# Loading the first batch's q and k by whole tokens and turning them on the matrix engine, with a new order of instructions, in a clustered-attention and SoLU feed-forward kernel

## The chip, the cores and the metric

One core of a Trainium2 chip runs the kernel. The metric is the time of one execution on the device in microseconds (us), the median of several runs; lower is better. The profile of one execution gives in addition the span, from its first to its last instruction, and for each engine what ran when. The engines are PE (matrix multiplication; PEld is its loading of the stationary operand), DVE (vector), ACT (activation), POOL and SP, which issues most transfers.

## The reference

```python
B, H, S, D = q.shape                      # 4, 8, 768, 64; 16 clusters a head
q_n = q / (norm(q) + 1e-6); k_n = k / (norm(k) + 1e-6); c_n = centroids / (norm(centroids) + 1e-6)
q_assign = argmax(einsum('bhsd,hcd->bhsc', q_n, c_n)); k_assign = argmax(einsum('bhsd,hcd->bhsc', k_n, c_n))
scores = where(q_assign[..., :, None] == k_assign[..., None, :], q @ k.T / 8, -1e9)
attn_out = softmax(scores) @ v
x = attn_out.transpose(0, 2, 1, 3).reshape(3072, 512)
h = x @ w_in                              # 512 to 1024
solu = h * softmax(h)
ln = (solu - mean(solu)) / sqrt(var(solu) + 1e-6) * g_ln
out = ln @ w_out                          # 1024 to 512
```

A key counts for a query only if both fall to the same centroid of their head. The sum over keys does not depend on the order of the keys, as long as k and v have the same order.

## The kernel before, in words

**Attention.** The work is cut into 4 batches and, in each, 4 pairs of heads. For each pair, q and k (`i` is 0 for q, 1 for k) are brought in as `raw`, laid out so that a transposition of 32x32 blocks on DVE (`turn`, L297) gives `xt`: 128 partitions, the 64 numbers of the one head above the 64 of the other, by 768 tokens in fp32. Four transfers fill a `raw` (`load`, L289), each of 96 KB in pieces of 32 numbers, that is 128 bytes. Two casts (`cast`, L303 on ACT, L305 and L307 on POOL), one for a head, write the bf16 operands `qbig` and `kbig`. The assignment of a pair goes through a chain: `clusters` (four fp32 products with the centroids into `csc`, L317, side by side in four strips of columns), `turn_back` (`cst`, L324), `assign_max` (`mx`, L329), `assign_hot` (`oh`, L333), `assign_turn` (`oht`, L339), all four on DVE, and eight small copies (`place`, L346, on DVE or POOL) that put the one-hot rows beside the numbers in `qbig` and `kbig`; four for each head of the pair. `blank` (L350) clears some rows for the second head. With these rows the score product itself carries the mask.

A unit is two times 128 queries of a head against its 768 keys. Its scores (`scores`, `sps`, L428) fill three PSUM banks, one at a time out of a ring of three; each bank goes through one exponential (`expo`, `e`, L433, ACT, 128x512), written to a ring of nine buffers; 12 products with v (`values`, `ops`, L445) end the unit and set its `e` buffers free. There are 24 units, so 72 exponentials, in a batch. Groups of two or three units share the single buffer `ops`; `normalise` (`den`, L457, and `x`, L468, on DVE) empties it, and only then may the next group's `values` begin. v comes in as `vf` (`load_v`, L355; pieces of 256 bytes) and is cast on POOL (L360).

**Feed-forward.** Each 128 tokens of `x` go through a block: a transposing transfer (`xT`, L476), `hps` (L509), maximum (`hm`, `nmax`), exponential (`e_sb`, L527, ACT), `u` (L533), a second transposing transfer (`uT`, L538), statistics on DVE, `yps` (L570), a scaling by `alpha` (`y`, L576 on ACT or L578 on DVE), and the store. There are 24 blocks. The weights are folded and centred once (`w_sum`, `mps`, `w_out_c`).

**Order.** Every step is entered with `add` as an operation with an engine, a cost, a key and what it needs; the class `Weave` lays them out in time with these costs and issues each engine's instructions in the order that it finds. Each engine works through its own list in that order and waits at the head of it. The tables `FEED`, `PAIR` and `KIND` shift the keys, `AWAY` names operations that go to another engine than their usual one. SP's list is one queue too: a transfer that waits for a buffer holds up those behind it. The pools: eight `raw`, six `xt`, three banks of the ring `hps`, six sets of `qbig`, `kbig` and v; pair number p of batch b uses set 4b + p modulo 6.

Of the kernel before, what the change touches and what calls it, by code (L numbers as in the profile page):

```python
# [892 lines left out]
```

## Time and profile before

| what | value |
|---|---|
| three runs | 251.89, 254.22, 254.29 us; median 254.22 |
| the profiled execution, its own time | 255.6 us |
| its span | 253.8 us |
| mean granted TensorE clock | 0.963 |
| bytes moved by DMA | 38.61 MB, 161592 of 166241 packets under 512 bytes |

Rows of the timeline read: start, duration, engine, line, operation, what it writes and reads with shapes, a count where like instructions are merged, and in brackets how long the engine stood idle before it and what ended that. Rows of the windows give the stretch, its length, busy time and count for PE, PEld, DVE, ACT and POOL, the granted clock of PE as a share of full speed, the mean busy share of the DMA engines and GB/s. Rows of groups give busy time in all, then the mean ns of one instruction.

### The profile page before, as it was taken

The page shows a single profiled execution, that of the slowest core. Times are in us where ns is not written, and L with a number is a line of the kernel's source. Part 1 is how long each engine was busy: PE and PEld are TensorE (multiplying, and loading weights), DVE is VectorE, ACT ScalarE, POOL GpSimd, SP SyncE. Part 2 cuts the span into 40 slices and gives each one's busy share as a digit, 9 for nine tenths or more (in the row PEclk, how much of TensorE's full clock was granted, in tenths as well). Part 3 has the DMA queues.
Part 4 walks back from the last instruction along what each step waited for, and adds up shares of the span by engine and source line. Part 5 has one row for each costly group of instructions (what it writes and reads, how often), then busy time and mean ns, then how long its engine had stood idle before and what let it go on. Part 6 is the DMA issues. An engine that isn't in the chain of part 4 may idle for free.

```text
span 253.8 us, 6697 instructions
## 1 busy us (share of the span) xinstructions
PE 223.8 (88%) x2336; PEld 140.0 (55%) x2336; DVE 215.8 (85%) x440; ACT 208.3 (82%) x427; POOL 128.3 (51%) x308
## 2 busy tenths in 40 slices
PE   0399848998799999999899999998999999999984
PEld 0046527764455566555466756665556567765441
DVE  5749895599979799998889999989999987899892
ACT  2259966998667899979899999999999779898632
POOL 5886893013446672556617583875543763023321
PEclk9999995799589999999999999999999999999998
DMA  9999999107869989999969999987799356465522
GB/s 152 181 173 206 361 363 147 26 4 114 144 128 204 182 144 156 197 196 119 156 123 220 131 228 141 198 160 110 137 176 188 108 76 97 116 83 123 149 83 83
DMA packets 166241, 38.61 MB, mean 152 GB/s; under 512 B 161592, under 2 KB 161600, under 8 KB 166208
## 3 DMA queue, kind: packets, MB, share of 16 engines
q1 hardware_dynamic: 163072, 37.80, 78.1%
q10 hardware_dynamic: 3136, 0.39, 1.0%
q8 instruction: 18, 0.29, 0.5%
q14 instruction: 15, 0.12, 0.2%
HBM read 23.11 MB, written 6.29 MB: 116 GB/s over the span
## 4 chain that ended last, share of the span: by engine, by line
PE 57%; DVE 14%; DMA 14%; ACT 8%; issue 5%; SPq 1%; ACTq 0%; DVEq 0%
PE sps L428 17%; PE hps L509 12%; PE yps L570 11%; PE ops L445 10%; DMA uT<-u 7%; ACT e L433 5%; PE csc L317 5%; DMA xT<-x 3%; DMA raw<-in_k_dram 3%; DVE u L533 3%; ACT e_sb L527 2%; DVE qbig L346 2%; DVE xt L297 2%; DVE x L468 1%; DVE bs L544 1%
## 5 line engine op out<-in xcount | busy, mean ns | idle before, releaser
L433 ACT ACTIVATE e<-sps 128x512 bf16<-128x512 f32 x288 | 149.8, 616 | 22.1 <-PE sps L428 17.5
L428 PE MATMUL sps<-qbig,kbig 80*128 80x256 bf16 (+3 forms) x648 | 105.4, 272 | 10.0 <-DVE qbig L346 6.2
L445 PEld LDWEIGHTS <-e 128*128 128x128 bf16 x1152 | 59.3, 101 | 24.8 <-issue 6.7
L428 PEld LDWEIGHTS <-kbig 80*128 80x128 bf16 (+1 forms) x648 | 51.6, 100 | 36.6 <-issue 13.2
L445 PE MATMUL ops<-v,e 128*128 128x65 bf16 x1152 | 66.9, 198 | 4.1 <-DVE x L468 2.9
L509 PE MATMUL hps<-w_in_sb,xT 128*128 128x512 bf16 x192 | 54.3, 386 | 1.7 <-DMA xT<-x 1.3
L570 PE MATMUL yps<-w_out_c,uT 128*128 128x512 bf16 x184 | 45.1, 379 | 2.7 <-DMA uT<-u 1.6
L527 ACT ACTIVATE e_sb<-hps,nmax 128x512 bf16<-128x512 f32 x48 | 33.1, 702 | 5.8 <-DVE nmax L520 5.7
L516 DVE TENSOR_REDUCE hm<-hps 128x1 f32<-128x512 f32 x48 | 32.2, 678 | 4.6 <-PE hps L509 4.2
L533 DVE TENSOR_TENSOR u<-e_sb,hps 128x512 bf16<-128x512 bf16 x48 | 31.8, 678 | 2.1 <-ACT e_sb L527 2.0
L297 DVE STREAM_TRANSPOSE xt<-raw 128x768 f32<-128x768 f32 x32 | 30.6, 966 | 1.4 <-DMA raw<-in_k_dram 1.2
L544 DVE BATCH_NORM_STATS2 bs<-u 128x6 f32<-128x512 bf16 x48 | 31.5, 677 | 0.1
L570 PEld LDWEIGHTS <-uT 128*128 128x128 bf16 x192 | 17.7, 97 | 22.1 <-DMA uT<-u 3.1
L558 POOL TENSOR_TENSOR esq<-esq,mv 128x1 f32<-128x1 f32 x24 | 4.5, 189 | 48.0 <-DVE mv L548 44.4
L346 POOL COPY kbig<-oht 32x192 f32<-32x192 f32 x49 | 17.4, 355 | 21.9 <-DVE oht L339 19.9
L305 POOL CAST qbig<-xt 64x768 bf16<-64x768 f32 x21 | 17.2, 820 | 21.6 <-DVE xt L297 19.3
L509 PEld LDWEIGHTS <-xT 128*128 128x128 bf16 x192 | 17.8, 99 | 11.7 <-issue 1.9
L307 POOL TENSOR_SCALAR kbig<-xt 64x768 bf16<-64x768 f32 x23 | 19.2, 837 | 6.7 <-DVE xt L297 4.7
L468 DVE TENSOR_TENSOR x<-ops,den 128x384 bf16<-128x384 f32 (+1 forms) x37 | 18.6, 504 | 1.3
L360 POOL CAST v<-vf 128x384 bf16<-128x384 f32 x32 | 15.7, 518 | 7.6 <-DMA vf<-in_v_dram 7.2
L317 PE MATMUL csc<-xt,c_bd 128*32 128x384 f32 x128 | 16.5, 542 | 2.1 <-DVE xt L297 2.0
L346 POOL COPY qbig<-oht 32x192 f32<-32x192 f32 x46 | 16.1, 351 | 2.3
(71 smaller groups left out, 179.1 us busy)
## 6 DMA issues: line engine op xcount, KB each, us to landing
vf<-in_v_dram SPq DMA_DIRECT2D x16, 384.0 KB, 4.9
out_dram<-y SPq DMA_DIRECT2D x24, 256.0 KB, 2.4
raw<-in_q_dram SPq DMA_DIRECT2D x62, 96.0 KB, 2.7
raw<-in_k_dram SPq DMA_DIRECT2D x62, 96.0 KB, 2.6
w_st<-in_moe_w_in_dram SPq DMA_DIRECT2D x4, 512.0 KB, 6.6
w_g<-in_moe_w_out_dram SPq DMA_DIRECT2D x4, 512.0 KB, 9.8
xT<-x SPq DMA_TRANSPOSE x23, 2.5
uT<-u SPq DMA_TRANSPOSE x22, 3.3
```

Source lines behind the costliest of these rows:

```text
L297: nc.vector.transpose(xt[:], raws[b, p, i][:].rearrange("p j c -> p (j c)"))
L317: nc.tensor.matmul(csc[c * NB:(c + 1) * NB, :], c_bd[:, p, :], xts[b, p, i][:, hf * HALF:(hf + 1) * HALF], tile_position=(0, c * NB))
L346: (nc.vector if e == "DVE" else nc.gpsimd).tensor_copy(dst, src)
L428: nc.tensor.matmul(sps_[n, k][:, c0:c0 + w], kbig[z][u, h % 2, bass.ts(kt, P)], qbig[z][u, h % 2, q0:q0 + w])
L433: nc.scalar.activation(es[n, k][:], sps_[n, k][:], Act.Exp, scale=exp_scale, bias=-exp_scale)
L445: nc.tensor.matmul(opss[g][:, s, :VW], es[n, k][:, c0:c0 + P], v1[slot(b, h // 2)][:, h % 2, kt, :VW], start=(kt == 0), stop=(kt == n_t - 1))
L509: nc.tensor.matmul(ff[f, "h", f2][:], xTs[f][:, dc, :], w_in_sb[:, dc, f2 * FF2:(f2 + 1) * FF2], start=(dc == 0), stop=(dc == n_dc - 1))
L516: nc.vector.tensor_reduce(ff[f, "hm"][:, f2:f2 + 1], ff[f, "h", f2][:], axis=AX, op=Alu.max)
L527: nc.scalar.activation(ff[f, "e"][:, f2, :], ff[f, "h", f2][:], Act.Exp, bias=ff[f, "nmax"][:], accum_out=ff[f, "esum"][:, f2:f2 + 1])
L533: nc.vector.tensor_tensor(ff[f, "u"][:, f2, :], ff[f, "e"][:, f2, :], ff[f, "h", f2][:], op=Alu.mult)
L544: nc.vector.bn_stats(ff[f, "bs"][:, f2, :], ff[f, "u"][:, f2, :])
L570: nc.tensor.matmul(ff[f, "y"][:], ff[f, "uT"][:, fc, :], w_out_c[:, fc, :], start=(fc == 0), stop=(fc == n_fc - 1))
```

## The change: what it does, and the diff

For the four pairs of batch 0 (`by_token`), q and k arrive by two transfers of 192 KB, one for a head, in pieces of 64 numbers (256 bytes): whole tokens, 128 partitions by six tokens. Partition p gets the tokens p, 128 + p, ... of q, and the tokens 6p to 6p + 5 of k. PE turns them, six 128x128 transpositions in fp32 for each of q and k (`turn_tokens`), three into one bank of the ring `hps`; a copy of 128x384 (`keep_tokens`) brings each bank to `xt`, eight of these copies on ACT and eight on DVE. v of batch 0 arrives by six tokens a partition, so that its keys have k's order; its pieces are 1536 bytes. Batches 1 to 3 load and turn as before.

The planner's tables are new throughout, and so is the order. Over the whole program, counted in the two lists: on DVE 8 fewer block transpositions of `raw`, 8 more copies, 12 fewer `place` copies (33 to 21), one more `blank`, two fewer scalings; on ACT 9 fewer casts (20 to 11), 8 more copies, two more scalings; on POOL 9 more casts, 12 more `place` copies, one fewer `blank`; on PE 48 more transpositions; on the two queues 16 transfers of batch 0's q and k instead of 32. `AHEAD` goes from 1 to 2, and a few costs that the planner assumes change.

In the diff the tables are cut to their first rows.

```diff
-    FEED = [2, -0.5, 8.5, -1.5, 1, 0, -5.5, 10, 6.5, 11.5, 12, 25, 14.5, 7.5, 8.5, 8.5, 6.5, 18,
+    FEED = [-1, 2, 2.5, 4.5, 5, 4, 6.5, 11, 18, 7.5, 8, 12.5, 7.5, 21, 10, 15.5, 16.5, 10.5,
...
-    AHEAD = 1
+    AHEAD = 2
...
+    n_turned = 1
+    def by_token(b):
+        return b < n_turned
+    def tokens(b, p, i):
+        return raws[b, p, i][:].rearrange("p j c -> p (j c)").rearrange("p (t e) -> p t e", t=n_t)
+    def load_tokens(b, p, i, hh, eng):
+        if hh == 0:
+            raws[b, p, i] = ld.tile([P, n_j, NB], F32, name="raw")
+        eng.dma_start(out=tokens(b, p, i)[:, :, hh * D:(hh + 1) * D],
+                      in_=SRC[i][b, 2 * p + hh].rearrange("(p t) d -> p t d" if i else
+                                                          "(t p) d -> p t d", p=P))
+    def turn_tokens(b, p, i, hf):
+        tps[b, p, i, hf] = ps_h.tile([P, HALF], F32, name="tps", tag="hps")
+        for t in range(n_t // 2):
+            nc.tensor.transpose(tps[b, p, i, hf][:, t * P:(t + 1) * P],
+                                tokens(b, p, i)[:, hf * (n_t // 2) + t, :], ident_f[:])
+    def keep_tokens(b, p, i, hf, e):
+        if hf == 0:
+            xts[b, p, i] = xtp.tile([P, S], F32, name="xt")
+        dst, src = xts[b, p, i][:, hf * HALF:(hf + 1) * HALF], tps[b, p, i, hf][:]
+        if e == "ACT":
+            nc.scalar.copy(dst, src)
+        else:
+            nc.vector.tensor_copy(dst, src)
...
-        nc.sync.dma_start(out=vf[:].rearrange("p h t d -> p (h t) d"),
-                          in_=v[b, 2 * p:2 * p + 2].rearrange("h (t p) d -> p (h t) d", p=P))
+        if by_token(b):
+            nc.sync.dma_start(out=vf[:].rearrange("p h t d -> p h (t d)"),
+                              in_=v[b, 2 * p:2 * p + 2].rearrange("h (p t) d -> p h (t d)", p=P))
+        else:
+            nc.sync.dma_start(out=vf[:].rearrange("p h t d -> p (h t) d"),
+                              in_=v[b, 2 * p:2 * p + 2].rearrange("h (t p) d -> p (h t) d", p=P))
...
-        for c in range(4):
-            load(0, 0, i, c, (nc.scalar, nc.sync)[c % 2])
+        for hh in range(2):
+            load_tokens(0, 0, i, hh, (nc.scalar, nc.sync)[hh])
...
+                if by_token(b):
+                    for hf in range(2):
+                        n2 = [f"ld{t}"]
+                        if len(ring_h) >= 3:
+                            n2.append(ring_h[-3])
+                        add(f"tp{t}.{hf}", "PE", 0.3, at - 15 + i,
+                            (lambda b=b, p=p, i=i, hf=hf: turn_tokens(b, p, i, hf)), n2,
+                            [last_tp[0]] if last_tp else [])
+                        last_tp[:] = [f"tp{t}.{hf}"]
+                        nm = f"xt{t}" if hf else f"xa{t}"
+                        e = on(nm, "ACT" if (b, p, i) == (0, 0, 1) else "DVE")
+                        add(nm, e, 0.53 if e == "DVE" else 0.46, at - 14 + i,
+                            (lambda b=b, p=p, i=i, hf=hf, e=e: keep_tokens(b, p, i, hf, e)),
+                            nd + [f"tp{t}.{hf}"] + [f"xa{t}"] * hf, af if hf == 0 else [])
+                        ring_h.append(nm)
```

The first place is PE's list at its start. `cps` is the turned centroids. Before:

```order
L888 UNCONDITIONAL_BRANCH
L629 MATMUL cps<-ident_f,c_n 128x128
L317 MATMUL csc<-xt,c_bd 32x384 x4
L428 LDWEIGHTS kbig_105
L428 MATMUL sps<-qbig_99,kbig_105 128x256
```

Now:

```order
L951 UNCONDITIONAL_BRANCH
L662 MATMUL cps<-ident_f,c_n 128x128
L303 MATMUL tps<-ident_f,raw 128x128 x12
L346 MATMUL csc<-xt,c_bd 32x384 x4
L303 MATMUL tps<-ident_f,raw 128x128 x9
L461 LDWEIGHTS kbig_105
L461 MATMUL sps<-qbig_99,kbig_105 128x256
```

The first pair's twelve transpositions stand behind `cps`, and nine of the second pair's twelve stand between the first assignment and the first scores.

The second place is DVE's list where the third and fourth pair of batch 0 are assigned (`kbig_107` and `qbig_101` belong to the third, `kbig_108` and `qbig_102` to the fourth). Before:

```order
L324 STREAM_TRANSPOSE cst<-csc 128x384
L329 TENSOR_REDUCE mx<-cst 128x24
L333 TENSOR_TENSOR oh<-cst,mx 128x384
L339 STREAM_TRANSPOSE oht<-oh 128x384
L346 COPY kbig_108<-oht 32x192
L346 COPY qbig_102<-oht 32x192 x3
L346 COPY qbig_101<-oht 32x192 x2
L346 COPY kbig_107<-oht 32x192
L346 COPY qbig_101<-oht 32x192
L457 RECIPROCAL den<-ops 128x6
L468 TENSOR_TENSOR x<-ops,den 128x6x64
```

Now:

```order
L368 STREAM_TRANSPOSE oht<-oh 128x384
L375 COPY kbig_107<-oht 32x192 x2
L490 RECIPROCAL den<-ops 128x6
L501 TENSOR_TENSOR x<-ops,den 128x6x64
L375 COPY qbig_101<-oht 32x192 x4
L379 MEMSET kbig_107 16x384
L313 COPY xt<-tps 128x384
L326 STREAM_TRANSPOSE xt<-raw 128x768
L490 RECIPROCAL den<-ops 128x6
L501 TENSOR_TENSOR x<-ops,den 128x6x64
L353 STREAM_TRANSPOSE cst<-csc 128x384
```

Before, two pairs' chains and eight `place` copies stood ahead of one `normalise`; now a `normalise` stands after two copies, the next comes ahead of the fourth pair's chain, and the fourth pair's eight `place` copies have gone to POOL.

The third place is SP's list where the weights (`w_st`, `w_g`) are fetched. The `raw` rows behind them are those of batch 1's first pair. Before:

```order
L355 DMA vf<-in_v_dram 128x12x64 x3
L376 DMA w_st<-in_moe_w_in_dram 128x1024 x4
L392 DMA w_g<-in_moe_w_out_dram 128x2x512 x4
L289 DMA raw<-in_q_dram 32x24x32 x4
L289 DMA raw<-in_k_dram 32x24x32 x4
```

Now:

```order
L318 DMA raw<-in_q_dram 32x24x32
L409 DMA w_st<-in_moe_w_in_dram 128x1024
L318 DMA raw<-in_q_dram 32x24x32 x3
L409 DMA w_st<-in_moe_w_in_dram 128x1024
L318 DMA raw<-in_k_dram 32x24x32
L409 DMA w_st<-in_moe_w_in_dram 128x1024
L318 DMA raw<-in_k_dram 32x24x32 x3
L409 DMA w_st<-in_moe_w_in_dram 128x1024
L388 DMA vf<-in_v_dram 128x12x64
L425 DMA w_g<-in_moe_w_out_dram 128x2x512 x4
```

Batch 1's first pair is now fetched among the first weights instead of behind all of them, and the v of batch 0's pairs, which stood in a row of three, each follows its own q and k.

More of the change, by code (lines that the diff above doesn't have):

```diff
@@ new lines @@
+    FEED = [-1, 2, 2.5, 4.5, 5, 4, 6.5, 11, 18, 7.5, 8, 12.5, 7.5, 21, 10, 15.5, 16.5, 10.5,
+        4.5, 7.5, 1.5, 0.5, 2.5, -0.5]
+    PAIR = [-27, 0, 1.5, -6, -9, -4.5, 0, -3, 19.5, -7.5, 1.5, -3, 21, 13.5, 21, 19.5]
+    KIND = {'cv': -23.5, 'wi': -36.0, 'tb': -12.0, 'ca': 16.0, 'xa': 20.0, 'N': -1.0, 'tp':
+        38.0, 'lg': 36.5, 'lo': -4.0, 'pl': -3.0, 'bl': 11.5, 'z': 35.5, 'xt': -1.0, 'lv': 1.5,
+        'ce': -1.0, 'oh': -1.0, 'su': 0.5, 'ld': 5.0, 'li': 4.0, 'ot': -1.0, 'cl': 0.5, 'mx':
+        0.5}
@@ L48 @@
-        pl0.1.1.1.0 pl0.2.0.1.1 pl0.2.1.0.0 pl0.2.1.0.1 pl0.2.1.1.0
+        bl0.0 ca0.0.0.0 ca0.0.0.1 pl0.0.0.0.0 pl0.0.0.0.1 pl0.0.1.0.0 pl0.0.1.0.1
+        pl0.2.1.0.1 pl0.2.1.1.1
     """.split(), "POOL"))
@@ L635 @@
     n_f = B * n_t
+    ring_h, last_tp = [], []
     for b in range(B):
@@ L643 @@
                 if (b, p) == (0, 0):
-                    add(f"ld{t}", "SP", 0.0, -100, lambda: None, move=2.6, lag=(2.4, 0.7))
+                    add(f"ld{t}", "SP", 0.0, -100, lambda: None, move=1.9, lag=(2.0, 0.7))
+                elif by_token(b):
+                    nd = []
+                    if seq >= 8:
+                        pb, pp = pairs[(seq - 8) // 2]
+                        nd = [f"xt{pb}.{pp}.{(seq - 8) % 2}"]
+                    prev = f"ld{pairs[(seq - 1) // 2][0]}.{pairs[(seq - 1) // 2][1]}.{(seq - 1) % 2}"
+                    for hh in range(2):
+                        nm = f"ld{t}" if hh else f"ld{t}.0"
+                        add(nm, "SP", 0.55, at - 40 + i,
+                            (lambda b=b, p=p, i=i, hh=hh: load_tokens(b, p, i, hh, nc.sync)),
+                            nd, [prev], move=0.95, bulk=True)
+                        prev = nm
                 else:
@@ L663 @@
                     nd += [f"ca{pt}.0", f"ca{pt}.1", f"cl{pb}.{pp}"]
-                af = [] if seq == 0 else [f"xt{pairs[(seq - 1) // 2][0]}."
-                                          f"{pairs[(seq - 1) // 2][1]}.{(seq - 1) % 2}"]
-                add(f"xt{t}", "DVE", 0.905, at - 14 + i, (lambda b=b, p=p, i=i: turn(b, p, i)), nd, af)
+                pt = "{}.{}.{}".format(*pairs[(seq - 1) // 2], (seq - 1) % 2)
+                af = [] if seq == 0 or by_token(b) else [f"xt{pt}"]
+                if by_token(b):
[13 more added lines that the diff above has]
+                        ring_h.append(nm)
+                else:
+                    add(f"xt{t}", "DVE", 0.905, at - 14 + i, (lambda b=b, p=p, i=i: turn(b, p, i)), nd,
+                        af)
                 for hh in range(2):
@@ L702 @@
             e = on("pl{}.{}.{}.{}".format(t, *x), e)
-            add("pl{}.{}.{}.{}".format(t, *x), e, 0.31 if e == "DVE" else 0.385, at - 8,
+            add("pl{}.{}.{}.{}".format(t, *x), e, 0.45 if e == "DVE" else 0.385, at - 8,
                 (lambda b=b, p=p, x=x, e=e: place(b, p, *x, e)), [f"ot{t}"] + behind(b, p, "S"))
@@ L847 @@
     for fc in range(n_fc):
-        add(f"su{fc}", "DVE", 0.66, 30 + fc, (lambda fc=fc: sum_w_out(fc)),
+        add(f"su{fc}", "DVE", 0.75, 30 + fc, (lambda fc=fc: sum_w_out(fc)),
             [f"lo{fc // 2}"] + ([f"su{fc - 1}"] if fc else ["gk"]))
-    add("me", "PE", 0.95, 36, mean_w_out, [f"su{n_fc - 1}", "sg"])
+    add("me", "PE", 0.95, 36, mean_w_out, [f"su{n_fc - 1}", "sg"] + ring_h[-3:-2], last_tp)
     for fc in range(n_fc):
```

23 lines of the change are left out of this document (7 added, 16 removed).

## The prediction

> **What bounds the kernel now.** I read the page's busy shares first, then busy time by stretches, and only then the timeline around the holes.
>
> ```profile
> PE 223.8 (88%) x2336; PEld 140.0 (55%) x2336; DVE 215.8 (85%) x440; ACT 208.3 (82%) x427; POOL 128.3 (51%) x308
> ...
> 13.80:35.60 21.80, 19.39 (x206) 11.75 (x205) 16.75 (x32) 19.72 (x38) 17.24 (x33) 1.00 1.09 278
> 35.60:39.40 3.80, 1.21 (x19) 1.00 (x18) 3.71 (x6) 0.03 (x2) 3.67 (x6) 0.71 1.11 240
> 39.40:47.00 7.60, 7.48 (x83) 5.97 (x81) 1.98 (x6) 6.32 (x12) 0.93 (x1) 0.50 0.67 121
> 47.00:62.00 15.00, 13.85 (x165) 9.28 (x164) 14.05 (x26) 13.46 (x27) 2.61 (x4) 0.99 0.28 47
> 62.00:74.00 12.00, 9.74 (x62) 5.48 (x63) 9.80 (x20) 7.81 (x17) 3.73 (x11) 0.72 0.74 130
> 74.00:240.00 166.00, 159.99 (x1752) 101.43 (x1750) 151.98 (x312) 152.77 (x322) 87.19 (x216) 1.00 0.84 150
> ```
>
> No engine alone is the bound. From 74 to 240 us three run together: PE 160 of 166, ACT 153, DVE 152. ACT can be read as a meter of progress, since the exponentials of attention are its work: it stands at 92% there. Before 74 us it stands lower. Idle on ACT: 2.1 us from 13.8 to 35.6, 3.8 to 39.4, 1.3 to 47, 1.5 to 62, 4.2 to 74, together 12.9 of 60.2 us; at the 8% of the middle it would be 4.8. So about 8 us lie open in the first batch. The first hole:
>
> ```profile
> 31.11 4.52 ACT L433 ACTIVATE e<-sps 128x512 bf16<-128x512 f32 x9
> 33.33 2.22 DVE L346 COPY qbig<-oht 32x192 f32<-32x192 f32 x5
> 38.09 0.56 DVE L468 TENSOR_TENSOR x<-ops,den 128x384 bf16<-128x384 f32 x1
> 38.70 2.14 PE L445 MATMUL ops<-v,e 128*128 128x65 bf16 x36 [2.59 <-DVE x L468]
> 39.40 1.57 ACT L433 ACTIVATE e<-sps 128x512 bf16<-128x512 f32 x3 [3.77 <-PE ops L445]
> ```
>
> Nine exponentials fill the nine `e` buffers. Their products with v wait until `normalise` empties `ops`, and on DVE that stands behind two pairs' chains and eight `place` copies. ACT waits 3.77 us. Then PE's granted clock is 0.50 until 47 us. The second hole is at the border to batch 1:
>
> ```profile
> 52.98 0.97 DVE L297 STREAM_TRANSPOSE xt<-raw 128x768 f32<-128x768 f32 x1
> 57.50 0.85 PE L317 MATMUL csc<-xt,c_bd 128*32 128x384 f32 x8
> 62.95 0.74 POOL L346 COPY kbig<-oht 32x192 f32<-32x192 f32 x2 [3.83 <-DVE oht L339]
> 64.89 2.40 PE L428 MATMUL sps<-qbig,kbig 80*128 80x256 bf16 x10 [2.01 <-DVE qbig L346]
> 65.57 0.60 ACT L433 ACTIVATE e<-sps 128x512 bf16<-128x512 f32 x1 [1.83 <-PE sps L428]
> ```
>
> Batch 1's first pair was fetched behind all weights; its first transposition is at 53, its assignment at 57.5, its copies at 63, its scores at 64.9. After this hole, too, the clock is granted by halves (0.72 on the mean of 62 to 74). The start is the third place:
>
> ```profile
> 5.31 0.47 PE L629 MATMUL cps<-ident_f,c_n 128*128 128x128 f32 x1 [5.31 <-DVE c_n L626]
> 6.31 1.84 DVE L297 STREAM_TRANSPOSE xt<-raw 128x768 f32<-128x768 f32 x2
> 9.75 0.58 DVE L324 STREAM_TRANSPOSE cst<-csc 128x384 f32<-128x384 f32 x1 [1.60 <-PE csc L317]
> 13.81 3.11 ACT L433 ACTIVATE e<-sps 128x512 bf16<-128x512 f32 x6 [4.78 <-PE sps L428]
> 19.40 6.60 ACT L433 ACTIVATE e<-sps 128x512 bf16<-128x512 f32 x13 [1.72 <-PE sps L428]
> ```
>
> **The change part by part.** *The transfers.* Three stretches give rates for three sizes of piece: 10 to 20 us only q and k (128 bytes), 23 to 26 mostly v (256 bytes), 28 to 36 weights.
>
> ```profile
> 10.00:20.00 10.00, 1.00 1.07 171
> 23.00:26.00 3.00, 1.00 1.31 232
> 28.00:36.00 8.00, 1.00 1.03 400
> ```
>
> A pair's q and k are 0.79 MB: 4.6 us at 171 GB/s, 3.4 at 232. Its v is 0.39 MB: 1.7 us at 232, 1.0 at 400. Over four pairs 4 x (1.2 + 0.7) = 7.6 us of transfer go. By itself this ends nothing sooner: in the whole run DVE's transpositions of `raw` waited 1.2 us for a transfer (the first row of groups below). I take 0 for it; if the first pair's transfers had been the limit, -1. What it pays for is the order. The first pair was there at 6.3; three pairs at 3.4 + 1.0 bring it to 19.5; batch 1's first pair (4.6 us at 171 GB/s) among four `w_st` of 0.52 MB (5.2 us at 400) is then there between 23 and 29 us.
>
> *The turn.* Its price is not shown, so it is bounded by these rows:
>
> ```profile
> 52.62 0.92 PE mps L405 x2
> 246.95 0.57 PE utp L495 x8
> 13.19 2.35 PE sps L428 x10
> 168.15 0.44 PE sps L428 x4
> ```
>
> The one fp32 product `mps` leaves two records of 512 columns, 0.92 us; `cps`, a turn, leaves one. So 128 columns of one record are 0.92 / 8 = 0.115 us. Eight bf16 turns take 0.57, that is 0.07 each; `cps` alone, with its start and end, 0.47. I take 0.115 at full clock (48 make 5.5 us) and keep 0.07 and 0.47 (3.4 and 22.7 us). PE stands idle 8.5 of the 60.2 us from 13.8 to 74 (51.67 busy), which hides 5.5; without this cover 5.5 would count whole. The `sps` rows give the factor for the slow stretch: 0.235 a record at 13 us against 0.11 later; a turn is then 0.23.
>
> *The start, walked through.* `cps` ends at 5.8. Three turns to a bank, 0.7 us: banks are ready near 6.5, 7.2, 7.9, 8.6. Each copy, 128x384 out of PSUM, is near the `x` row below (0.56). ACT, DVE, ACT, ACT take them; the last ends near 9.1. Before, the two block transpositions ended at 6.31 + 1.84 = 8.15, and `cst` began 1.6 later; now it begins at 10.7. From `cst` to the first exponential it was 13.81 - 9.75 = 4.06, so 14.7: **+0.9** (bounds -0.5, if the copies overlap better, and +4.5, worked out under the rivals). But PE works from 5.3 on, first at `cps` and 21 turns. Before, PE's products took twice their time from 13.2 to about 20, and ACT lost 0.16 + 1.72 us to it. Of these 1.9 I take **-0.7**, as I can't see whether a turn brings the clock up as a product does.
>
> ```profile
> L297 DVE STREAM_TRANSPOSE xt<-raw 128x768 f32<-128x768 f32 x32 | 30.6, 966 | 1.4 <-DMA raw<-in_k_dram 1.2
> L468 DVE TENSOR_TENSOR x<-ops,den 128x384 bf16<-128x384 f32 x22 | 12.3, 558 | 0.8
> L303 ACT ACTIVATE qbig<-xt 64x768 bf16<-64x768 f32 x11 | 9.4, 850 | 4.1 <-DVE xt L297 4.0
> L305 POOL CAST qbig<-xt 64x768 bf16<-64x768 f32 x21 | 17.2, 820 | 21.6 <-DVE xt L297 19.3
> L346 POOL COPY qbig<-oht 32x192 f32<-32x192 f32 x46 | 16.1, 351 | 2.3
> L346 DVE COPY qbig<-oht 32x192 f32<-32x192 f32 x18 | 6.8, 380 | 0.4
> L576 ACT ACTIVATE y<-yps,alpha 128x512 f32<-128x512 f32 x18 | 12.4, 691 | 5.0 <-PE yps L570 4.0 <-POOL es L554 0.8
> ```
>
> *The first hole.* ACT passes an exponential in 0.51 (6.60 / 13). From 14.7, with one cast and four copies on the way, the 37th is due near 36. By then the third pair must be placed. Its copies to `xt` are ACT's, after the 18th and 19th exponential (near 27); `csc`, chain and `oht` end near 31; two `place`, `normalise` at 32 to 33, four `place` more: 34.5. So this `normalise` is no longer behind the fourth pair, and the hole closes with 1.5 us to spare. The fourth pair's last copy on ACT follows the 37th exponential; its `oht` is near 40, its eight copies on POOL take 8 x 0.35: 43.5, due near 46. I take **-3.2** of the 3.8, and for the clock that then stays up **-0.8** of 1.3.
>
> *The second hole.* Batch 1's first pair is now turned on DVE between two `normalise` of batch 0 and placed on POOL behind the fourth pair, some 5 us before it is due. But `hps` of the first feed-forward block has moved back by ten banks of scores in PE's list, so its chain still has to start up. Of the 4.2 us I take **-1.6**.
>
> *The loads.* ACT: -9 x 0.85 + 8 x 0.5 + 2 x 0.69 = -2.3 us. DVE: -8 x 0.97 + 8 x 0.56 - 12 x 0.38 and two scalings less: about -9. POOL: +9 x 0.82 + 12 x 0.35 = +11.6, at 51% of the span. Where PE, ACT and DVE are equally full, PE's products don't get fewer, so I take **-0.8** (bounds 0 and -4).
>
> Sum: 0.9 - 0.7 - 3.2 - 0.8 - 1.6 - 0.8 = **-6.2 us**. For the profiled execution (span 253.8, its own time 255.6) that is 249.4; it lay 1.4 above the median of the three runs, 254.22, and from that the forecast is **248.0 us**.
>
> A rule stands against the start. The Trainium skill, "TensorE: Matmul & The Clock Gate", Part 4 (PE-mode transpose), says that transposes do not count as PE activity for the clock gate and gives some 275 ns for one of 128x128 bf16 in a kernel. The trace has 70 ns in the row of `utp`, so the figure does not hold here; about the clock no row can tell. By the figure 48 turns would be 13.2 us, 4.7 more than PE's idle time hides, and the sum would be -1.5.
>
> **The rivals.**
> 1. *The turns don't bring the clock up.* For it: only products ended the slow stretches here. Against: none of the rows. Then the first scores run at half speed: the -0.7 falls away, the second pair's nine turns cost 9 x 0.115 more, ahead of scores, and the half speed lasts into the second pair: about +2.2. 250.2 us. The skill's rule above would make this one.
> 2. *POOL becomes the bound.* Its list holds, ahead of the fourth pair's copies, casts of weights and of batch 1's first pair and v, so a late transfer or 20% dearer copies eat the 2.5 us of slack. For it: POOL was busy 17.24 of 21.8 us already with less work. Then ACT waits some 3 us near 46, and the clock halves again (0.8 + 0.5): 248.0 + 4.3 = 252.3.
> 3. *The turn is dear, the one that ends slower.* At `cps`'s own 0.47, twelve turns take 5.6 us, `xt` is ready at 12, nine more turns (4.2) stand ahead of the first scores, first exponential at 18.3 (+4.5). The other 27 take 12.7 us against 8.5 idle: +4.2. Less the 2.1 for the half clock (first hole and border), less 0.8 for loads, less about 2 of the holes that remain: +3.8, 258. It decides from the price at which idle PE is used up and the gain gone: (8.5 + 6.2) / 48 = 0.31 us a turn.
> 4. *The middle shortens too.* If ACT and not PE paces it, 5 us of ACT and DVE work moved from there to POOL count by 4 instead of 0.8, and the border closes wholly (-1.4): 243.4. For it: ACT's 92% over so long a stretch; against: PE is at 160 of 166.
>
> **How the numbers follow.** Forecast 0.42, rival one 0.15, two 0.18, three 0.13, four 0.12. This kernel's measurement can tell about 1%, that is 251.7 and 256.8. Faster by over 1%: 0.42 + 0.13 (most of one) + 0.12 + 0.01 (little of two) = 0.68. Within 1%: 0.14 of two, 0.02 of one, 0.02 of three = 0.18. Slower: 0.11 of three and 0.03 of two, 0.14. The range, 242.5 to 256.5, takes in all of four and two, and leaves out most of three and what lies below four.
>
> **What would show it.** Right: in the new profile the exponentials run on past 36 us with no wait of over 1 us on `ops`; the granted clock has no 0.5 between 37 and 47; batch 1's first scores start before 60; ACT idle from the first exponential to 74 us falls from 12.9 to about 6; a turn's record, back to back, is near 0.12. Wrong: the first exponential after 16; ACT waiting at the fourth pair with POOL as releaser; turns over 0.3; or the holes gone and the stretch after 74 us longer by as much, which would mean that PE's work, not the holes, sets the end.

## The result and the profile after

| | before | after |
|---|---|---|
| median of four runs, us | 254.09 (251.89 to 254.29) | 243.46 (242.70 to 244.73) |
| profiled execution, own time / span, us | 255.6 / 253.8 | 243.92 / 242.1 |

The ratio is 0.9606, with a 95% interval of 0.9536 to 0.9675: faster by 10.6 us. The forecast was 6.2 us (248.0 us), and the stated range, 242.5 to 256.5 us, holds the result near its lower end. In some of the kernels below single runs took over 1.5% longer than the fastest run of the same kernel; the ratios leave those out. The page of the changed kernel, its busy shares and its row of granted clock:

```profile
PE 219.2 (91%) x2354; PEld 142.1 (59%) x2384; DVE 207.4 (86%) x427; ACT 205.5 (85%) x428; POOL 141.6 (58%) x328
...
PEclk9979999999999999999999999999999999999999
```

DVE has lost 8.4 us of work and ACT 2.8; POOL has gained 13.3 (forecast -9, -2.3, +11.6). The same stretches as before (columns: stretch, length, busy time of PE, PE's weight loads, DVE, ACT, POOL, then granted clock, DMA share, GB/s):

```profile
13.80:35.60 21.80, 20.57 (x249) 15.50 (x250) 15.18 (x36) 19.74 (x40) 14.70 (x25) 0.92 1.00 249
35.60:39.40 3.80, 3.69 (x37) 1.69 (x33) 3.66 (x8) 3.26 (x7) 2.31 (x4) 1.00 1.01 370
39.40:47.00 7.60, 7.05 (x101) 4.99 (x100) 7.32 (x14) 7.02 (x14) 7.07 (x15) 1.00 0.97 177
47.00:62.00 15.00, 13.85 (x172) 9.29 (x172) 14.49 (x26) 13.65 (x28) 11.98 (x19) 1.00 0.95 153
62.00:74.00 12.00, 11.09 (x108) 6.94 (x108) 11.50 (x25) 10.30 (x23) 5.68 (x17) 1.00 0.76 134
```

ACT's idle time from 13.8 to 74 is 2.1 + 0.5 + 0.6 + 1.4 + 1.7 = 6.2 us, where it was 12.9; 1.0 of the 2.1 lies ahead of the first exponential. The stretch from 35.6 to 39.4, which was a hole, is full, and the clock is no longer halved from 39.4 to 47 nor after 62. ACT's exponentials in the timeline:

```profile
14.77 1.57 ACT L466 ACTIVATE e<-sps 128x512 bf16<-128x512 f32 x3 [3.63 <-PE sps L461]
...
29.55 7.46 ACT L466 ACTIVATE e<-sps 128x512 bf16<-128x512 f32 x15 [0.30 <-PE sps L461]
...
44.60 10.39 ACT L466 ACTIVATE e<-sps 128x512 bf16<-128x512 f32 x21 [0.35 <-PE sps L461]
55.32 2.06 ACT L466 ACTIVATE e<-sps 128x512 bf16<-128x512 f32 x4 [0.33 <-PE sps L461]
57.98 3.00 ACT L466 ACTIVATE e<-sps 128x512 bf16<-128x512 f32 x6
62.19 0.60 ACT L466 ACTIVATE e<-sps 128x512 bf16<-128x512 f32 x1 [1.22 <-PE sps L461]
```

No wait ahead of an exponential from 15 to 63 us is over 1.3 us, and the group at 29.55 runs on past 36. These rows also give a measure that lines the two kernels up by progress instead of by the clock on the wall: a pair has 18 exponentials, so the 1st, 19th, 37th and 55th begin batch 0's pairs, and the 73rd begins batch 1. Where such a one lies inside a group, it starts at the group's start plus its place by the group's mean (the group at 55.32 begins with the 71st; the 73rd is at 55.32 + 2 x 0.515 = 56.35), which is right to some 0.3 us. Counted along the whole timeline of both kernels:

| exponential | 1st | 37th | 55th | 73rd | 91st | 145th | end of span |
|---|---|---|---|---|---|---|---|
| before, us | 13.81 | 39.40 | 50.56 | 65.57 | 82.95 | 124.25 | 253.8 |
| after, us | 14.77 | 36.51 | 47.07 | 56.35 | 72.17 | 114.04 | 242.1 |
| difference | +1.0 | -2.9 | -3.5 | -9.2 | -10.8 | -10.2 | -11.7 |

Nearly all is won when batch 1's second pair begins; more than half of it, 7.3 us, from the 55th to the 91st exponential, and 5.7 of these before the 73rd. Four of the stretches between these points, before:

```profile
13.81:39.40 25.59, 20.59 (x223) 12.74 (x222) 20.45 (x37) 19.75 (x39) 20.91 (x38) 0.96 1.09 272
50.56:65.57 15.01, 12.03 (x139) 7.78 (x138) 13.77 (x29) 11.92 (x25) 4.96 (x11) 0.96 0.44 67
65.57:82.95 17.38, 17.38 (x147) 10.20 (x146) 15.26 (x29) 13.51 (x26) 8.11 (x21) 0.83 0.86 166
82.95:124.25 41.30, 38.23 (x409) 23.55 (x408) 37.59 (x74) 37.22 (x79) 24.82 (x56) 1.00 0.95 166
```

and after:

```profile
14.77:36.51 21.74, 20.90 (x254) 15.57 (x252) 15.10 (x35) 20.65 (x42) 14.74 (x23) 0.93 0.99 250
47.07:56.35 9.28, 8.50 (x115) 6.05 (x115) 8.80 (x16) 8.95 (x20) 8.75 (x15) 1.00 0.90 142
56.35:72.17 15.82, 14.54 (x140) 8.76 (x143) 15.58 (x31) 13.10 (x29) 7.49 (x19) 1.00 0.84 140
72.17:114.04 41.87, 39.22 (x431) 25.16 (x437) 39.10 (x74) 39.62 (x81) 29.06 (x65) 1.00 0.98 182
```

Over the border (second and third rows) ACT's idle time falls from 3.1 + 3.9 to 0.3 + 2.7 us, that is by 3.9. Its work there falls by 3.4: two casts of batch 1's first pair (1.7 us) are gone to POOL for good, and a third cast (0.8) and a scaling `y` (0.7) are done later. The fourth rows show where work went: ACT does 2.4 us more there, mostly scalings (five for two), and the stretch is only 0.6 longer, since its idle time falls by 1.8.

### The profile page after: what moved, and what is told of

Its sections match the earlier page's. It is cut to its first block, busy times and chain, and to the rows that moved or that the text cites. A ratio compares the mean times of both kernels' runs of the same rounds, so it can differ in the third digit from the quotient of the medians.

```text
span 242.1 us, 6729 instructions
## 1 busy us (share of the span) xinstructions
PE 219.2 (91%) x2354; PEld 142.1 (59%) x2384; DVE 207.4 (86%) x427; ACT 205.5 (85%) x428; POOL 141.6 (58%) x328
## 4 chain that ended last, share of the span: by engine, by line
PE 65%; DVE 11%; DMA 9%; ACT 7%; issue 6%; POOL 1%; SPq 0%; ACTq 0%; DVEq 0%; POOLq 0%
PE sps L461 17%; PE yps L603 16%; PE hps L542 12%; PE ops L478 11%; DMA uT<-u 6%; ACT e L466 5%; PE csc L346 4%; PE tps L303 2%; DVE w_out_c L441 2%; DMA xT<-x 2%; DVE x L501 1%; DVE hm L549 1%; DVE qbig L375 1%; ACT e_sb L560 1%; DMA c_all<-in_centroids_dram 1%
## 5 line engine op out<-in xcount | busy, mean ns | idle before, releaser
L461 PE MATMUL sps<-qbig,kbig 80*128 80x256 bf16 (+3 forms) x648 | 101.1, 262 | 6.2 <-POOL qbig L375 2.1
L478 PEld LDWEIGHTS <-e 128*128 128x128 bf16 x1152 | 57.5, 98 | 21.4 <-issue 3.8
L478 PE MATMUL ops<-v,e 128*128 128x65 bf16 x1152 | 65.6, 194 | 1.0 <-DVE x L501 0.6
L542 PE MATMUL hps<-w_in_sb,xT 128*128 128x512 bf16 x172 | 49.0, 379 | 1.9 <-DVE w_out_c L441 0.5
L375 POOL COPY kbig<-oht 32x192 f32<-32x192 f32 x57 | 21.2, 372 | 20.6 <-DVE oht L368 18.1
L603 PEld LDWEIGHTS <-uT 128*128 128x128 bf16 x192 | 17.7, 98 | 20.1 <-DMA uT<-u 3.5
L334 POOL CAST qbig<-xt 64x768 bf16<-64x768 f32 x25 | 21.2, 848 | 7.1 <-ACT xt L311 5.9
L336 POOL TENSOR_SCALAR kbig<-xt 64x768 bf16<-64x768 f32 x28 | 23.7, 847 | 2.7 <-DVE xt L313 1.3
L326 DVE STREAM_TRANSPOSE xt<-raw 128x768 f32<-128x768 f32 x24 | 22.1, 950 | 0.1
L375 POOL COPY qbig<-oht 32x192 f32<-32x192 f32 x50 | 18.4, 367 | 2.5
L609 ACT ACTIVATE y<-yps,alpha 128x512 f32<-128x512 f32 x20 | 13.7, 687 | 7.0 <-POOL alpha L593 3.7
```

What stands on the lines that cost most here:

```text
L326: nc.vector.transpose(xt[:], raws[b, p, i][:].rearrange("p j c -> p (j c)"))
L336: nc.gpsimd.tensor_scalar(dst[r, hh, :], xt[r], scalar1=inv_C, scalar2=1.0, op0=Alu.mult, op1=Alu.mult)
L375: (nc.vector if e == "DVE" else nc.gpsimd).tensor_copy(dst, src)
L461: nc.tensor.matmul(sps_[n, k][:, c0:c0 + w], kbig[z][u, h % 2, bass.ts(kt, P)], qbig[z][u, h % 2, q0:q0 + w])
L478: nc.tensor.matmul(opss[g][:, s, :VW], es[n, k][:, c0:c0 + P], v1[slot(b, h // 2)][:, h % 2, kt, :VW], start=(kt == 0), stop=(kt == n_t - 1))
L542: nc.tensor.matmul(ff[f, "h", f2][:], xTs[f][:, dc, :], w_in_sb[:, dc, f2 * FF2:(f2 + 1) * FF2], start=(dc == 0), stop=(dc == n_dc - 1))
```

## The experiments

Eleven other kernels and the changed one once more, each beside runs of the kernel before on its own chip. I compare ratios to the kernel before; 0.001 is 0.25 us, and the intervals leave a difference of two kernels uncertain by some 2 us. The changed kernel, run again with the last group of three, is the yardstick.

> The changed kernel itself once more, as the measure for the three beside it. 0.955 to 0.966 of the kernel before.

Measured: 244.59 us (243.82 to 248.22), ratio 0.961 [0.9562, 0.9658]. The first result stands.

**Is it the order or the loading?** The change has two halves: other tables, and the first batch's loading with the turn. One kernel has the first alone, one the second. Each runs an order with a loading that it was not laid out for.

```
-    n_turned = 1
+    n_turned = 0
...
-        for hh in range(2):
-            load_tokens(0, 0, i, hh, (nc.scalar, nc.sync)[hh])
+        for c in range(4):
+            load(0, 0, i, c, (nc.scalar, nc.sync)[c % 2])
...
-                    add(f"ld{t}", "SP", 0.0, -100, lambda: None, move=1.9, lag=(2.0, 0.7))
+                    add(f"ld{t}", "SP", 0.0, -100, lambda: None, move=2.6, lag=(2.4, 0.7))
...
```

> The new tables alone: no batch is loaded by tokens, batch 0 is loaded by 128-byte pieces and turned by DVE as before, and the planner orders with the new tables and costs. Theory (the gain is the closed holes, and the holes are matters of order; the turn by itself only makes room): about 246 to 249, the first hole still small, DVE fuller in batch 0. Rival (the turn is what closes them, since 16 copies replace eight block transpositions of DVE and the transfers get faster): 251 to 255, holes of 3 us back.

Measured: 254.72 us (10 runs), ratio 0.9986 [0.9951, 1.0021]: nothing is gained. The theory was half right: the order alone does close the first hole (ACT's longest wait ahead of an exponential from 20 to 45 us is 1.06 us, and the 37th is at 35.3 us), but it doesn't win the time. The rival named the time rightly and not the reason, since no hole of 3 us is back there. By the count of exponentials this kernel begins batch 1 early, the 73rd at 56.7 us, but the 91st is at 73.9 and the 145th at 121.4, where the changed kernel has 72.2 and 114.0. Its stretches:

```profile
45.28:56.70 11.42, 9.36 (x114) 7.09 (x110) 10.77 (x17) 9.30 (x20) 10.58 (x17) 0.85 0.88 216
56.70:73.85 17.15, 13.53 (x134) 8.01 (x133) 15.47 (x30) 12.57 (x29) 6.50 (x16) 1.00 0.98 148
73.85:121.35 47.50, 42.86 (x460) 26.49 (x465) 42.31 (x81) 41.53 (x85) 33.70 (x80) 1.00 1.03 184
```

From the 91st to the 145th it takes 47.5 us against 41.9. What differs there is the supply of data: the DMA share is at 1.03, and of POOL's casts of v the groups say (idle time of POOL just before them at the end):

```profile
L393 POOL CAST v<-vf 128x384 bf16<-128x384 f32 x32 | 15.6, 517 | 27.1 <-DMA vf<-in_v_dram 26.8
```

That is 26.8 us of waiting for v in nine places, where the changed kernel has:

```profile
L393 POOL CAST v<-vf 128x384 bf16<-128x384 f32 x32 | 15.4, 505 | 8.5 <-DMA vf<-in_v_dram 5.2
```

So the gain in batch 0 was given back later, at late transfers by these rows; that they alone cost it is argued, not shown.

The other half: the new loading and the turn, with the tables, `AHEAD` and the two costs of before (the lines below are a part of the edit).

```
-    FEED = [-1, 2, 2.5, 4.5, 5, 4, 6.5, 11, 18, 7.5, 8, 12.5, 7.5, 21, 10, 15.5, 16.5, 10.5,
+    FEED = [2, -0.5, 8.5, -1.5, 1, 0, -5.5, 10, 6.5, 11.5, 12, 25, 14.5, 7.5, 8.5, 8.5, 6.5, 18,
...
-    AHEAD = 2
+    AHEAD = 1
...
-            add("pl{}.{}.{}.{}".format(t, *x), e, 0.45 if e == "DVE" else 0.385, at - 8,
+            add("pl{}.{}.{}.{}".format(t, *x), e, 0.31 if e == "DVE" else 0.385, at - 8,
...
```

> The turn alone: batch 0 by tokens, turned by PE, but tables and planner's costs of the kernel before. Theory (order closes the holes): 250 to 254, with the wait at the border to batch 1 still there, because its first pair is fetched late. Rival (the turn closes them): 244 to 247.

Measured: 276.18 us, ratio 1.0836 [1.0779, 1.0892], slower by 8%, above both expectations. ACT's timeline has two long waits:

```profile
29.06 4.51 ACT L468 ACTIVATE e<-sps 128x512 bf16<-128x512 f32 x9 [2.68 <-PE sps L463]
41.46 3.82 ACT L468 ACTIVATE e<-sps 128x512 bf16<-128x512 f32 x7 [7.88 <-PE sps L463]
```

and POOL's tells what the second is:

```profile
34.02 0.55 POOL L377 COPY kbig<-oht 32x192 f32<-32x192 f32 x1
34.64 1.04 POOL L414 CAST w_in_sb<-w_st 128x1024 bf16<-128x1024 f32 x1
35.62 0.36 POOL L377 COPY qbig<-oht 32x192 f32<-32x192 f32 x1
...
37.92 2.31 POOL L338 TENSOR_SCALAR kbig<-xt 64x768 bf16<-64x768 f32 x2
40.29 0.41 POOL L381 MEMSET kbig<- 16x384 f32 x1
```

POOL's list alternates casts of weights with the copies on which scores wait, and puts two casts ahead of the clearing of `kbig` (L381); for this PE stood 6.7 us, until 40.75. This is the prediction's second rival as it looks when it happens. Neither half is faster by itself as it stands here; the change is the two together. Whether an order laid out anew for the old loading would win was not tried.

**The turn's price.** Every one of the 48 turns is done twice.

```
-        for t in range(n_t // 2):
+        for t in list(range(n_t // 2)) * 2:
```

> The changed kernel with each of the 48 transpositions made twice, into the same place. Measured so far: 1.28 us for nine, 0.14 each at full clock, so 48 more are 6.8 us of PE in batch 0, of which 12 lie ahead of the first assignment (12 x 0.21 = 2.5 us at half clock). Theory (ahead of the first assignment the turn lies on the path, later idle PE hides it): +2.5 to +4, 246 to 247.5. Rival (all of it counts): +6.8, 250. Rival (hidden throughout): within 0.5 of 243.5.

Measured: 249.26 us, ratio 0.9781 [0.9734, 0.9828]: 4.3 us more than the changed kernel, somewhat more than expected and less than the 48 x 0.142 = 6.8 that the turns cost on PE. By the count of exponentials only a part of it falls where the turns are: the 1st comes 1.1 us later, the 91st 1.3 us (73.47 for 72.17), so idle PE in batch 0 hides the rest there. The 145th is 2.8 us late and the end 4.8, over a stretch in which no turn stands; why the lateness grows there stays open. PE's timeline:

```profile
12.00 2.19 PE L303 MATMUL tps<-ident_f,raw 128*128 128x128 f32 x18
15.43 0.81 PE L461 MATMUL sps<-qbig,kbig 80*128 80x256 bf16 x6 [1.24 <-POOL qbig L375]
```

Eighteen turns in 2.19 us are 0.122 each (both means hold the last turn's end and a slow first one; in the trace the turns then start 0.11 us apart), and six products of scores take 0.135 each, full speed, after a gap of 1.24 us.

**Turns and the clock.** In the changed kernel the first scores ran at half speed, though the turns before them did not. PE's timeline there:

```profile
5.96 2.93 PE L303 MATMUL tps<-ident_f,raw 128*128 128x128 f32 x12
8.81 2.12 PE L346 MATMUL csc<-xt,c_bd 128*32 128x384 f32 x8
10.87 1.28 PE L303 MATMUL tps<-ident_f,raw 128*128 128x128 f32 x9
14.30 1.29 PE L461 MATMUL sps<-qbig,kbig 80*128 80x256 bf16 x6 [2.15 <-POOL qbig L375]
```

The products with the centroids take 0.265 each here and 0.106 later (eight in 0.85), and the twelve turns ahead of them 0.244, so PE still ran slowly; the nine turns behind them took 0.142 each, not twice that. Then PE waits 2.15 us and six products take 0.215 each. Either the turns don't count for the clock, or the wait had lowered it again. An experiment fills the wait with 15 further turns, whose results nobody reads.

```
-        for t in range(n_t // 2):
+        for t in list(range(n_t // 2)) * (6 if (b, p, i, hf) == (0, 1, 1, 0) else 1):
```

> The changed kernel with 15 further transpositions in the second pair's third bank, the same data into the same place: about 2.1 us of PE work in the hole from 12.2 to 14.3 us, after which the trace showed records at twice their time until 17.6. Theory (a hole of 2 us on PE brings the half clock, and turns count as work): the first scores run at full speed, the exponentials lose about 1 us less by 20 us, 0.5 to 1.5 us faster than the changed kernel. Rival (turns don't count for the clock): no faster, and 0 to 0.5 slower through the later first scores.

Its timeline of PE:

```profile
10.71 3.30 PE L303 MATMUL tps<-ident_f,raw 128*128 128x128 f32 x24
14.20 0.82 PE L461 MATMUL sps<-qbig,kbig 80*128 80x256 bf16 x6 [0.20 <-POOL qbig L375]
```

The same six products take 0.137 each. The stretch from 14 to 18 us, first the changed kernel, then this one:

```profile
14.00:18.00 4.00, 3.70 (x28) 3.01 (x28) 2.31 (x5) 2.79 (x6) 3.69 (x9) 0.57 1.17 286
```

```profile
14.00:18.00 4.00, 3.70 (x43) 2.32 (x42) 2.12 (x5) 3.38 (x7) 3.69 (x9) 1.00 1.11 268
```

The clock is 1.00 where it was 0.57, and by the 55th exponential the profile is 1.2 us ahead (45.9 against 47.1). The six runs of this kernel have a mean clock of 0.993 to 1.000, those of the changed kernel beside them 0.985 to 0.993. Without the turns PE would have no work for 3.4 us in either kernel, from the products with the centroids to the first scores. So turns do keep the clock up, and it was the wait that lowered it. One reservation: in the kernel with the old tables PE waits 2.26 us at this place, too, and no half clock follows. The time is 244.25 us, ratio 0.957 [0.9509, 0.9631]; beside 0.961 [0.9562, 0.9658] on the same chip that can't be told from no change, and the 1.2 us is the profile's word alone, though the 55th lies between 46.7 and 48.9 in seven other profiles that have the changed kernel's lists up to nearly there.

**Do the transfers matter?** The prediction set their own worth at nothing. Here batch 0's q and k come in pieces of 128 bytes again, two transfers for one, at the same places of the list.

```
-        eng.dma_start(out=tokens(b, p, i)[:, :, hh * D:(hh + 1) * D],
-                      in_=SRC[i][b, 2 * p + hh].rearrange(...))
+        for c in range(2):
+            eng.dma_start(out=tokens(b, p, i)[:, :, hh * D + c * NB:hh * D + (c + 1) * NB],
+                          in_=SRC[i][b, 2 * p + hh, :, c * NB:(c + 1) * NB].rearrange(...))
```

> The changed kernel, in which each transfer of q and k of batch 0 is cut into two of 32 columns, so that the pieces are of 128 bytes again and twice as many; layout, turn and order as changed. Theory (the transfers end nothing sooner by themselves, as forecast): 243 to 245, 1 us later at the start at most. Rival (the room on the queue carries the closed holes): holes come back near 27 to 40 us, 246 to 249.

Measured: 250.22 us, ratio 0.9806 [0.9761, 0.985], 5 us more. Little of it is where I had looked, at batch 0's own pairs. The count of exponentials has the 73rd at 57.67 (1.3 later than the changed kernel), the 91st at 77.73 (5.6 later). Its stretch between the two:

```profile
57.67:77.73 20.06, 16.02 (x140) 9.11 (x143) 15.99 (x32) 13.21 (x30) 8.61 (x20) 0.91 0.95 159
```

20.1 us instead of 15.8, with the same 13.1 to 13.2 of ACT's work in it and a clock of 0.91. The lateness jumps between the 79th (1.4 us) and the 85th (5.5). Its timelines of SP's queue, PE and ACT give the reason:

```profile
38.14 3.11 SPq L426 DMA_DIRECT2D w_g<-in_moe_w_out_dram  x4
...
60.87 1.30 SPq L510 DMA_TRANSPOSE xT<-x  x1
```

```profile
64.17 3.03 PE L543 MATMUL hps<-w_in_sb,xT 128*128 128x512 bf16 x7 [2.82 <-DMA xT<-x]
```

```profile
67.71 0.60 ACT L467 ACTIVATE e<-sps 128x512 bf16<-128x512 f32 x1 [5.31 <-PE sps L462]
```

In the changed kernel the same rows of SP's queue stand some 8 us earlier, and `hps` at 60.02:

```profile
30.55 3.87 SPq L425 DMA_DIRECT2D w_g<-in_moe_w_out_dram  x4
...
52.13 1.29 SPq L509 DMA_TRANSPOSE xT<-x  x1
```

The first transposing transfer of `xT` stands in SP's queue behind all of batch 1's `raw` transfers for the second and third pair, and these behind the weights. A queue that is 8 us late behind batch 0's loads makes the feed-forward late at 60 us: PE waits 2.8 us for `xT`, the clock falls, and ACT waits 5.3. The edit halves the pieces and also gives SP 14 more transfers to issue, at some 0.4 us each where the queue is free (a `raw` at 26.21: 0.41), so near 6 of the 8 us by this estimate; which of the two makes the queue late, no run separates.

How much lateness does the queue bear? Two further kernels ask. One changes batch 0's v alone, to pieces of 256 bytes, with k's tokens in q's order so that the sums stay the same.

```
-        if by_token(b):
+        if False:
...
-                      in_=SRC[i][b, 2 * p + hh].rearrange("(p t) d -> p t d" if i else
+                      in_=SRC[i][b, 2 * p + hh].rearrange("(t p) d -> p t d" if i else
```

> The changed kernel with v of batch 0 in pieces of 256 bytes as before the change, and the tokens of k in q's order for that: 4 x 0.7 = 2.8 us more of transfer in the first 20 us, nothing else. Theory (transfers of batch 0 hold SP's queue, and the transposing transfers of the first feed-forward block stand at its end): +1.5 to +3 against the changed kernel. Rival (only the narrow pieces of q and k matter, or there is slack of 3 us): within 0.7.

Measured: 244.95 us, ratio 0.961 [0.9553, 0.9668]: no price. In its timeline the first `xT` is fetched at 53.12 us and `hps` starts at 61.02, both 1.0 us later than in the changed kernel, and the 145th exponential only 0.5 later. A queue late by one microsecond costs nothing that can be measured, one late by 8 costs 5; where between them the price begins was not tried.

The other goes the other way: v of batches 1 to 3, too, by six tokens in a partition, with k's tokens reordered to match.

```
-        if by_token(b):
+        if True:
...
+                in_=SRC[i][b, 2 * p + c // 2, :, (c % 2) * NB:(c % 2 + 1) * NB]
+                .rearrange("(a i t) c -> i t a c", i=NB, t=n_t))
```

> The changed kernel with the v of batches 1 to 3 also by six tokens a partition (pieces of 1536 bytes instead of 256), and the keys of k fetched in the same order, by 128-byte pieces as before. Theory (the transfers are on the path: with pieces of 128 bytes in batch 0 the time rose by about 5 us for about 5 us of transfer): 12 x 0.7 = 8.4 us of transfer less where the DMA engines are 0.9 to 1.1 busy, 1 to 4 us faster than the changed kernel. Rival (after the first batch a late transfer is hidden by the eight raw buffers): within 0.7 us.

Measured: 246.83 us (244.4 to 249.42), ratio 0.9663 [0.9601, 0.9725]: not faster; by the ratio 1.3 us slower, if anything. From 80 to 200 us the DMA share falls from 0.84 to 0.78, but PE (113.7 and 113.5 us busy) and ACT (113.7 and 113.1) get no further for it. So behind batch 0 fewer packets bring nothing in this kernel, though the DMA engines are busy 84% there. The edit fetches k in another order, too; that this cost what v gained isn't excluded. Whether the 1.3 us are real, and why, stays open.

**What is the middle bound by?** The prediction gave lighter loads 0.8 us, its fourth rival 4. Four kernels each add some 6 to 7 us of work in batches 1 to 3 to one engine, by doing a thing twice.

ACT's eight casts:

```
+        for _ in range(2 if b else 1):
             nc.scalar.activation(dst[r, hh, :], xt[r], Act.Copy, scale=inv_C if i else 1.0)
```

> The changed kernel, in which ACT makes each of its eight casts in batches 1 to 3 twice, to the same place: 8 x 0.84 = 6.7 us more work on ACT, the order untouched. Theory one (ACT paces the stretch after 74 us, so its lighter load came back whole, about 2.8 us): the time goes from 243.5 to 249 to 250. Theory two (PE paces it, as the forecast had it with 0.8 of 2.3): at most +2, below 245.5.

Measured: 247.08 us, ratio 0.9679 [0.9612, 0.9747], about 1.8 us more for 6.7 of work, nearer to theory two than to theory one.

Seven of DVE's block transpositions:

```
+        for _ in range(2 if i == 0 and (p % 2 == 0 or (b, p) == (2, 1)) else 1):
             nc.vector.transpose(xt[:], raws[b, p, i][:].rearrange("p j c -> p (j c)"))
```

> The changed kernel, in which DVE makes seven of its block transpositions of q in batches 1 to 3 twice: 7 x 0.95 = 6.7 us more on DVE. Theory one (ACT paces the stretch after 74 us; DVE is busy 140 of 154 us there, as much as ACT): under 2 us, up to 245.5. Rival (all three full engines stand in one chain, each of them counts): 3 to 6 us more, 246.5 to 249.5.

Measured: 246.43 us, ratio 0.9654 [0.9587, 0.9721], about 1.1 us more for 6.65.

The products with the centroids, for nine pairs:

```
-        for c in range(4):
+        for c in list(range(4)) * (2 if b and p < 3 else 1):
```

> The changed kernel, in which PE makes the four products with the centroids twice for nine pairs of batches 1 to 3: 9 x 0.78 = 7.0 us more on PE. Theory one (ACT paces): +1 to +2.5, since PE at 147 of 154 us has little room, 244.5 to 246. Theory two (PE paces): +6 to +7, 249.5 to 250.5.

Measured: 252.18, 247.29, 251.68 and 252.19 us; the runs disagree, so there is no ratio. By the kernel before on that chip (255.34) the changed kernel would be at 0.961 x 255.34 = 245.4, so three runs cost 6.3 to 6.8 for 7.0 of work, and one 1.9. The profile is of one of the three, and not all of its lateness is the products': its 19th exponential is already 1.3 us late (28.06 us for 26.79), before any product is made twice. What PE's work costs stays open between 1.9 and 6.8.

Seven casts of POOL:

```
+        for _ in range(2 if b and hh == 1 and (b, p) != (1, 0) else 1):
             nc.gpsimd.tensor_copy(dst[r, hh, :], xt[r])
```

> The changed kernel, in which POOL makes seven of its casts of q in batches 1 to 3 twice: 7 x 0.83 = 5.8 us more on POOL, which is busy 88 of 154 us in that stretch. Both theories: no change beyond 0.5 us, 243 to 244. If the work that moved to POOL had a price of its own (POOL's list in order, and the copies and casts behind it), +2 to +4.

Measured: 244.40 us, ratio 0.9572 [0.95, 0.9644]: nothing for 5.8.

Added work of ACT and DVE counts by a fifth to a quarter (uncertain by 2 us in 6.7, so by 0.3), POOL's not at all. That is nearer to the prediction's 0.8 than to the 4 of 5 us in its fourth rival, as far as added work tells what work taken away is worth. That PE paces the middle is not shown.

## Why the prediction came out as it did

By its own steps, with the terms put beside the count of exponentials (the sum measured is that of the two profiled executions; the medians differ by 10.6):

| term | forecast, us | stretch | measured, us |
|---|---|---|---|
| start | +0.9 | to the 1st | +1.0 |
| half clock at the start, first hole | -0.7 - 3.2 = -3.9 | 1st to 37th | -3.9 |
| half clock behind it | -0.8 | 37th to 55th | -0.6 |
| border to batch 1 | -1.6 | 55th to 91st | -7.3 |
| lighter loads | -0.8 | 91st to the end | -0.9 |
| sum | -6.2 | | -11.7 |

- **The start** was walked through rightly: the first exponential at 14.77 for 14.7. The turn cost 0.142 in a group of nine and 0.122 in one of eighteen, for 0.115; the two bounds, 0.07 and 0.47, were far off.
- **Its half clock** gave what was said, but not in the way that was said. From its first exponential to 35.6 us ACT idles 1.1 us now and 2.1 before. The turns did raise the clock, by 11 us; what I had not seen is that PE would then wait 2.15 us for the first `qbig`, after which it is halved once more, for a shorter time. Filling that wait brought the 1.00. The agreement at -3.9 is in part luck: by the first rows of the stretches above ACT's idle time falls from 5.8 to 1.1 us, that is by 4.8 (3.8 of it the first hole, 1.0 the start), and its work grows by 0.9, since four copies out of PSUM (2.2 us) stand there for one cast (0.85). The forecast had 3.2 and 0.7, and that work not at this place.
- **A rule spoke against the turn.** The length of a turn's record and its price are two things here:

```profile
L303 PE MATMUL tps<-ident_f,raw x48: 270/273/447, 6.0 to 32.1; 128*128 128x128 f32 x48
```

  These are the shortest, the median and the longest record in ns. But the records overlap, so a turn costs PE 0.122 to 0.142 us, and with turns in PE's gap the clock stays at 1.00. The Trainium skill, "TensorE: Matmul & The Clock Gate", Part 4 (PE-mode transpose), has a transpose of 128x128 bf16 at some 275 ns in a kernel and says that it doesn't count as busy for the clock. The trace agrees with the first as a length, though the turns are fp32; the prediction's answer, 70 ns in the row of `utp`, set a price against it. The second doesn't hold for these turns; whether they run in the mode that the page means, the trace doesn't show. The first rival, which the rule would have made, falls with it.
- **The first hole** closed as forecast, by the order: the third pair was placed in time, and no exponential waits long on `ops`. With the old pieces it closes too (the 37th at 37.39 us), and with the new tables alone. But the slack was smaller than said. The fourth pair's eight copies on POOL were to end at 43.5, due near 46. POOL's timeline:

```profile
41.04 1.15 POOL L334 CAST qbig<-xt 64x768 bf16<-64x768 f32 x1
42.15 0.95 POOL L393 CAST v<-vf 128x384 bf16<-128x384 f32 x2
43.16 0.75 POOL L375 COPY kbig<-oht 32x192 f32<-32x192 f32 x2
43.95 0.85 POOL L375 COPY qbig<-oht 32x192 f32<-32x192 f32 x2
44.84 0.72 POOL L375 COPY kbig<-oht 32x192 f32<-32x192 f32 x2
45.63 0.94 POOL L375 COPY qbig<-oht 32x192 f32<-32x192 f32 x2
```

  They end at 46.6, with a cast and a v of batch 1 ahead of them, half a microsecond before the 55th exponential at 47.07. The second rival was that close, and the kernel with the turn and the old tables shows in full what it looks like.
- **The border is the term that was mis-sized**: -1.6 forecast, -7.3 measured, 5.7 us more, where the whole sum was short by 5.5. The mechanism was right: batch 1's first pair is there early, and its scores run on from batch 0's. I had taken -1.6 of 4.2 because `hps` moved back and its chain "still has to start up". It did move back, to 60.02 us from 58.92, but ACT has batch 1's exponentials to run meanwhile, so the start-up costs it 1.2 us at 62.19 and no more. Of the 7.3, 3.9 us is ACT's idle time. The other 3.4 is work that no longer stands there, which the forecast had not counted at this place at all: two casts gone to POOL, and a cast and a scaling done later, where ACT had 1.8 us more idle than now. PE's clock, 0.83 from the 73rd to the 91st exponential before and 1.00 now, is in it too; how the 7.3 divide among these causes no run separates.
- **The transfers at 0** were the other step that failed. The rows were read for who waits on `raw`, and DVE's transpositions had waited 1.2 us in all. The queue's last customer is another: `xT`. With the old pieces the gain is halved (-5 of -10), by SP's queue running 8 us late, not through batch 0's q and k. The forecast said that the transfers pay for the order; it should have asked what the order costs without them.
- **The loads** came out at the size said behind the 91st exponential, but that shows little: from there to the end the changed kernel takes 169.9 us in the one profile and 171.2 in the other, the kernel before 170.9. Two casts more are in the border's 3.4. The fourth rival's number, 243.4, is the nearest to the result, and half of its reason, that the border closes wholly, is what happened; its larger half, ACT's and DVE's work counting nearly in full, is not what the doubled work shows.
- **Third rival**: the turn is not dear. At twice the price the kernel is still 2.2% faster than before.

No version tried clearly beats the changed kernel.

## What to carry to other kernels

When a hole at a border between stages closes, ask what the waiting engine will run instead of what chain has yet to start, and count work that leaves the place as well as idle time. Line two profiles up by counting the same operation along the bounding engine: a table of a few such points shows which term of a forecast was wrong, where times on the wall do not. Price a faster transfer by everything that stands behind it in its queue, to the last user; and try an order and the loading it was made for apart and together, since each half here, in the form tried, was worth nothing or less.

## What the runs showed of the hardware that was not expected

- In nine profiles of kernels that begin with the turns PE waits 2.0 to 2.5 us ahead of the first scores. In eight a stretch at half speed follows, but not always at once: in the changed kernel 0.2 us after the work resumes (clock 0.57 from 14 to 18 us), in its second profile (the run once more), after a wait of 2.50 us, some 2 us later (six products at 0.135 us each, then a clock of 0.50 from 16 to 18 us). It lasts to between 18 and 20.7 us, and where it lasts past 20, the 19th exponential comes at 27.8 to 28.1 us, elsewhere at 26.5 to 26.8. So profiles of one order differ by 1.3 us from this alone. In the ninth (turn, old tables; 2.26 us) none follows, nor after the wait of 1.24 us in the kernel with doubled turns.
- In the first 14 us the granted clock's column says 1.00 in both kernels, while products with the centroids take 0.265 us each in the changed kernel for 0.106 later: at the start of these runs the durations tell the speed, the column doesn't.
- From 10 to 17 us the changed kernel moved 288 GB/s, with q and k in pieces of 256 bytes and two transfers of v in pieces of 1536 among them; with q and k in pieces of 128 bytes and one such transfer of v it was 175.
